# Attention scores as three one-pass products of split queries and keys, and fewer tiles for incoming weight words

## The chip, the cores and the metric

The kernel runs on one core of one Trainium2 chip. The metric is the device time of one execution in microseconds (us), median of three runs. A core has five engines that matter here: TensorE (PE) for matrix products, VectorE (DVE), ScalarE (ACT), GpSimd (POOL), and SyncE (SP), which starts the transfers (DMAs). Each works through its own instructions in the order in which they stand and waits for others by semaphores.

## The reference

Attention over 8 batches, 12 heads, 448 positions and head size 64, with the scores mixed across heads before the softmax and the weights mixed across heads after it; then a feed-forward block on all 3584 tokens.

```python
scores = scale * np.matmul(q, k.transpose(0, 1, 3, 2))
scores = np.einsum('bhij,hg->bgij', scores, w_pre)
scores = scores - np.max(scores, axis=-1, keepdims=True)
attn = np.exp(scores)
attn = attn / (np.sum(attn, axis=-1, keepdims=True) + 1e-09)
attn = np.einsum('bhij,hg->bgij', attn, w_post)
out = np.matmul(attn, v)
...
a = x @ w1
b = x @ w2
h = a * b @ w3
return (h @ w_out).astype(np.float32)
```

The weights of the feed-forward block arrive as 64-bit words and are turned into 32-bit floats on the chip.

## The kernel before, in words

The order of the work is written out by hand. `run` goes through 366 steps (`n`), two steps for each pair of tiles of ten query rows. In an even step the pair's row maxima (`largest`, L227, DVE) and exponentials (`exp`, L235, ACT) are issued; in an odd step PE gets the products with V (`av`, L301, when they are due), the head mixing after the softmax of the pair before (`post`, L260, tiles `pso`), the head mixing before the softmax of the next pair (`mix`, L220, tiles `psm`), and then the score units that a table `qks` puts into this step (`qk`, L174, tiles `psq`). The rest of the step's PE time goes to the feed-forward block (`eg`, `eo`, `e`, `e1o` to `e3o`; L522, L553, L702), so many matmuls in each step as a table `share` says. Those are 128x448 products of operands split into a rounded high part and a low rest (type fp32r): three one-pass products (`PAIRS`) instead of one full fp32 product. The program is thus one fixed order on each engine.

A **score unit** `(b, p, c)` computes, for batch `b` and the two heads of pair `p`, 128 rows of queries (`c` 0 to 2) against all 448 keys; `c` 3 takes the last 64 rows of two pairs at once. Head 0 has its 64 elements in rows 0 to 63 of the tile `kq`, head 1 in rows 64 to 127. Before, a unit is four fp32 matmuls with 64 rows and 64 columns of the array each: two heads times two halves of 64 queries. An fp32 matmul stands as two records in the trace, so a unit is eight records of `psq`. ACT copies its two banks out (`st`, L179 and L180), and SP stores them (`raw_d<-st`). SP loads `kq` (`load_kq`, L157) six steps ahead into four buffers.

The **weight words**: `ask_words` (L103) starts on SP the load of one piece of words (`cs<-w`) and appends it to a list; `converting` takes the oldest, lets ACT square the upper halves (`square`, L110, tile `cm`), DVE assemble the floats (L121 to L124), and, a step later, ACT and POOL split them (`two_parts`, L129 and L130), after which SP stores the parts (`w_d<-wu`, L425). The first 40 pieces (`5 * KF`) belong to the folded weights and are done by step 50; 32 pieces of `w1` and `w2` follow. The list is filled up to `DEEP` (5) pieces in five buffers of tag `s`. Later `sums` uses buffers of the same tag for combinations of weights: ACT casts (L483), POOL subtracts (L484), SP stores (`s_d<-s`, L486).

Of the kernel before, what the change touches and what calls it, by code (L numbers as in the profile page):

```python
# [15 lines left out]
B, H, S, D = 8, 12, 448, 64  # L16
DM, FF = 768, 1024
HP = H // 2
# [3 lines left out]
QT, NJ = 128, 4  # L22
GB = 15
NG = NB // GB
KF, K1 = FF // 128, DM // 128
IH = IB // 2
HK = H * IH
PP = 64
# [3 lines left out]
CW = 384  # L32
DH = DM // 2
LATE = 2 * NB + GB + 2
PAIRS = ((0, 0), (0, 1), (1, 0))
N_UP, NS = 20, 50
DEEP = 5
ONE = 2


# [10 lines left out]
class Kernel:  # L51
# [43 lines left out]

    def ask_words(self, depth):

        while len(self.asked) < depth and self.sources:
            src, n = self.sources.pop(0), self.n_words
            s = self.cs.tile([128, CW, 2], I32, tag="s", name=f"cs{n}", bufs=DEEP)  # L100
            a, k = src.shape[1], src.shape[2] // 2
            s = s[:, :a * k]
            self.nc.sync.dma_start(s.rearrange("p (a n) b -> p a (n b)", a=a), src)  # L103
            self.asked.append(s)
            self.n_words += 1
# [26 lines left out]
    def converting(self, jobs, late=False):  # L132
# [22 lines left out]
    def load_kq(self, b, p):  # L155
        t = self.kp.tile([128, 2 * S], F32, tag="kq", name=f"kq{b}_{p}", bufs=4)
        self.nc.sync.dma_start(t, self.kq[b, p].rearrange("p a j -> p (a j)"))  # L157
        self.kqs[b, p] = t

    def parts(self, b, p, c):  # L160
        pairs = ((p, 2 * c), (p, 2 * c + 1)) if c < 3 else ((p - 1, 6), (p, 6))
        if b == 0:
            return [(self.kqs[0, p], j * PP + S * (j > 1), QT) for p, j in pairs]
        return [(self.kqs[b, p], j * PP, S) for p, j in pairs]

    def qk(self, b, p, c, banks):


        nc = self.nc
        ps = [self.bank(i, f"psq{b}_{p}_{c}_{s}")[:, :S] for s, i in enumerate(banks)]  # L170
        for z, (t, q, k) in enumerate(self.parts(b, p, c)):
            for s in range(2):
                rows = slice(s * D, (s + 1) * D)
                nc.tensor.matmul(ps[s][z * PP:(z + 1) * PP], t[rows, q:q + PP], t[rows, k:k + S], start=True, stop=True)  # L174
        if b == c == 0:
            st = self.sz[:, 2 * p:2 * p + 2]
        else:
            st = (self.qp if b == 0 and p % 2 else self.kp).tile([128, 2, S], F32, tag="st", name=f"st{b}_{p}_{c}", bufs=2)
        nc.scalar.copy(st[:, 0], ps[0])  # L179
        (nc.vector.tensor_copy if b == c == 0 else nc.scalar.copy)(st[:, 1], ps[1])  # L180
        raw = self.raw_d[b]
        if c == 3:
            def store():
                for z in range(2):
                    nc.sync.dma_start(raw[3 * QT:, 2 * (p + z) - 2:2 * (p + z)], st[z * PP:(z + 1) * PP])
            return store
        n = QT if b or c else FIRST
        return lambda: nc.sync.dma_start(raw[c * QT:c * QT + n, 2 * p:2 * p + 2], st[:n])
# [280 lines left out]
    def sums(self, w, f, k):  # L469


        nc, n = self.nc, k * 128
        y = self.ys.pop((w, f))[:, :, :n]

        def sum(out, a, b, op):
            nc.vector.tensor_tensor(out, a, b, op=op)

        def split(m, i):
            s = self.cs.tile([128, CW, 2], I32, tag="s", name=f"s{w}_{f}_{m}", bufs=DEEP)
            s = s.rearrange("p n b -> p (n b)").bitcast(F32)  # L480
            dst, x = self.s_d[w][m][f].rearrange("p (t n) -> p t n", t=2), y[:, i]
            hi, lo = s[:, :n], s[:, n:2 * n] if w < 2 else x
            nc.scalar.copy(hi.bitcast(F32R), x)  # L483
            nc.gpsimd.tensor_tensor(lo.bitcast(F32R), x, hi, op=ALU.subtract)  # L484
            if w < 2:
                self.later.append(lambda: nc.sync.dma_start(self.s_d[w][m][f], s))  # L486
            else:
                self.later.append(lambda: nc.sync.dma_start(dst[:, 0], hi))
                self.later.append(lambda: nc.sync.dma_start(dst[:, 1], lo))

        def first():
            sum(y[:, 0:2], y[:, 0:2], y[:, 2:4], ALU.subtract)

        def second():
            sum(y[:, 1:3], y[:, 1:3], y[:, 0::3], ALU.add)

        def third():
            sum(y[:, 3], y[:, 3], y[:, 0], ALU.subtract)
# [242 lines left out]
    def run(self):  # L741
        nc, tc = self.nc, self.tc
# [33 lines left out]
        w = self.kp.tile([128, 2, S], F32, tag="st", name="wpre_s", bufs=2)[:, 0, :PP]  # L776
# [29 lines left out]

        loads, qks, avs = {}, {}, {}
        for n, u in enumerate([(0, p, c) for c in (1, 2) for p in range(HP)] + [(0, p, 3) for p in range(1, HP, 2)]):  # L810
            qks[n] = [u]
        for b in range(1, B):
            first, per = (11, 28 / 21) if b == 1 else ((b - 1) * NB - 6, NB / 21)
            units = [(b, p, c) for g in range(0, HP, 2) for p, c in [*itertools.product((g, g + 1), range(3)), (g + 1, 3)]]
            for i, (b, p, c) in enumerate(units):
                n = int(first + i * per) | (b > 1)
                qks.setdefault(n, []).append((b, p, c))
                if c == 0:
                    loads.setdefault(max(n - 6, 0), []).append((b, p))
        for b in range(B):  # L820
            for a in range(NG):
                for g in range(HP):
                    n = (b * NB + (a + 1) * GB + 3) | 1
# [65 lines left out]
        for n in range(N + 6):  # L889
# [4 lines left out]
            if n == SWITCH:  # L894
                assert done == total
                next(background, None)
                self.do_ends()
                self.do_soon()
                self.do_later()
                assert not fold_pieces  # L900
                self.close("fp")
                self.wp = self.pool("wp", 5, side="right")
                self.up = self.pool("up", 1, side="right")
                self.xp.append(self.pool("xp1", 1, side="right"))
                background, total, done = self.experts(phases), (E_1 + E_2) * ONE + P_1 * (B - ONE) // 2, 0
# [18 lines left out]
            m, odd = divmod(n, 2)  # L924
# [44 lines left out]
            self.do_ends()  # L969
            if not odd and m < SETS:  # L970
                self.exp(m)
            advance(now - now // 2)
            for x in avs.get(n, []):
                self.av(*x)
# [33 lines left out]
def words(w):  # L1008

    import numpy as np  # L1010
    return np.ascontiguousarray(w).view(np.int64)


def layouts(inputs):
    import numpy as np
    q, k, v = inputs["q"], inputs["k"], inputs["v"]
    qt = q.transpose(0, 1, 3, 2).reshape(B, HP, 2, D, S)
    kt = k.transpose(0, 1, 3, 2).reshape(B, HP, 2 * D, S)
    kq = np.ascontiguousarray(np.stack([qt.reshape(B, HP, 2 * D, S), kt], axis=3))
# [32 lines left out]
```

## Time and profile before

| what | value |
|---|---|
| median of 3 runs | 1441.87 us (1441.68 to 1443.87) |
| the profiled execution, its own time | 1437.83 us |
| its span, first to last instruction | 1436.1 us |
| mean granted TensorE clock | 0.986 |
| busy: PE, DVE, ACT, POOL | 1382.4, 741.1, 832.4, 620.3 us |
| from 220 to 376 us: 31 squares of weight words, DMA share | 17.64 us busy, 0.95 |

A row of the profile's groups gives line, engine, operation, output and inputs, the array's rows and columns for PE, and the count; then busy time and mean duration in ns. A row of the timeline gives start, duration, the same names and, in brackets, idle time ahead of it with what ended it. Matmuls are pipelined: what one costs is the distance between starts, not its duration.

### The profile page before, as it was taken

How to read it: one execution, taken by the hardware profiler on the slowest of the kernel's cores; microseconds unless marked ns; L12 is line 12 of the kernel's file. 1: busy time of each engine (PE TensorE's matmuls, PEld its weight loads, DVE VectorE, ACT ScalarE, POOL GpSimd, SP SyncE). 2: the span in 40 equal slices, each digit the busy share in tenths (PEclk: the TensorE clock that was granted, in tenths of full speed). 3: DMA queues.
4: the chain of work that ended last, by engine and by line, in shares of the span. 5: the costliest groups of instructions: out<-in, count | busy, mean ns of one | idle time of the engine just before them, and what ended most of it. 6: DMA issues, size and time to landing. Idle time of an engine off the chain costs nothing.

```text
span 1436.1 us, 45775 instructions
## 1 busy us (share of the span) xinstructions
PE 1382.4 (96%) x18684; PEld 1055.2 (73%) x18684; DVE 741.1 (52%) x1497; ACT 832.4 (58%) x1952; POOL 620.3 (43%) x754
## 2 busy tenths in 40 slices
PE   5889999999999999999999999999999999999998
PEld 2457786776677667776777777777777777899988
DVE  6867566767544544432444436334444446345563
ACT  4867666777766666665656556556555445422231
POOL 2433233434433544532345336334335446446693
PEclk7989999999999999999999999999999999999999
DMA  8998789999999999999989979799879757698775
GB/s 294 366 326 279 236 270 322 320 312 317 324 286 348 355 356 330 362 346 349 287 275 290 320 259 280 249 323 354 288 229 281 241 177 223 195 337 270 231 232 171
DMA packets 203761, 416.87 MB, mean 290 GB/s; under 512 B 20528, under 2 KB 120112, under 8 KB 203472
## 3 DMA queue, kind: packets, MB, share of 16 engines
q1 hardware_dynamic: 203552, 413.94, 87.6%
q8 instruction: 149, 2.44, 0.7%
q14 instruction: 60, 0.49, 0.1%
HBM read 279.77 MB, written 134.09 MB: 288 GB/s over the span
## 4 chain that ended last, share of the span: by engine, by line
PE 82%; DMA 8%; DVE 4%; ACT 2%; issue 1%; POOL 1%; SPq 0%; DVEq 0%; POOLq 0%; ACTq 0%
PE e L702 21%; PE psa L301 11%; PE pso L260 10%; PE psm L220 9%; PE psq L174 7%; PE eg L522 5%; PE psf L360 4%; PE eo L553 4%; PE e2o L702 4%; PE e1o L702 4%; PE e3o L702 4%; DMA wu<-w_d 3%; DMA r<-raw_d 2%; DMA raw_d<-st 2%; ACT e L235 1%
## 5 line engine op out<-in xcount | busy, mean ns | idle before, releaser
L247 POOL TENSOR_SCALAR w<-wpo,ri 128x60 f32<-128x60 f32 x360 | 180.7, 518 | 485.1 <-DVE ri L245 465.3
L227 DVE TENSOR_REDUCE mn<-psm 128x1 f32<-128x448 f32 x360 | 207.7, 618 | 321.6 <-PE psm L220 321.3
L274 ACT COPY mt<-pso 128x480 f32<-128x480 f32 x352 | 197.9, 621 | 185.8 <-PE pso L260 185.6
L702 PE MATMUL e<-eh,wu 128*128 128x448 f32 x1008 | 296.8, 371 | 6.4 <-DVE c L656 3.2
L235 ACT ACTIVATE e<-psm,mn 128x448 f32<-128x448 f32 x360 | 226.8, 643 | 7.9 <-DVE mn L227 7.9
L702 PEld LDWEIGHTS e<-eh,wu 128*128 128x128 f32 x1008 | 187.5, 188 | 52.2 <-issue 26.8
L260 PEld LDWEIGHTS pso<-w,e 60*64 60x64 f32 x10080 | 175.2, 135 | 51.0 <-issue 42.5
L220 PE MATMUL psm<-r,wsc 60*64 60x448 f32 (+1 forms) x1440 | 191.2, 550 | 19.1 <-DVE cx L124 8.3
L260 PE MATMUL pso<-w,e 60*64 60x60 f32 x10080 | 199.1, 224 | 0.4 <-ACT mt L274 0.3
L702 PE MATMUL e<-el,wu 128*128 128x448 f32 x504 | 186.9, 371 | 0.0
L301 PE MATMUL psa<-mt,v 128*64 128x150 f32 (+1 forms) x2304 | 156.9, 292 | 4.1 <-ACT st L179 4.1
L301 PEld LDWEIGHTS psa<-mt,v 128*64 128x64 f32 x2304 | 143.6, 137 | 20.1 <-ACT st L179 6.7
L174 PE MATMUL psq<-kq 64*64 64x448 f32 x1176 | 154.6, 542 | 2.4 <-ACT st L179 2.4
L656 DVE TENSOR_TENSOR c<-c,e 128x448 f32<-128x448 f32 x168 | 101.7, 618 | 87.7 <-PE e L702 82.9
L179 ACT COPY st<-psq 128x448 f32<-128x448 f32 x162 | 86.4, 533 | 73.7 <-ACT mt L274 34.1
L522 PE MATMUL eg<-xh,wu 128*128 128x448 f32 x384 | 119.2, 381 | 6.3 <-DMA wu<-w_d 6.3
L641 POOL TENSOR_TENSOR el<-x,eh 128x448 fp32r<-128x448 f32 x90 | 103.7, 1170 | 32.8 <-ACT eh L640 29.9
L702 PEld LDWEIGHTS e<-el,wu 128*128 128x128 f32 x504 | 94.6, 188 | 22.5 <-issue 14.1
L174 PEld LDWEIGHTS psq<-kq 64*64 64x64 f32 x1176 | 60.8, 135 | 56.4 <-issue 28.8
L522 PEld LDWEIGHTS eg<-xh,wu 128*128 128x128 f32 x384 | 71.9, 190 | 38.7 <-issue 24.0
L244 DVE TENSOR_SCALAR sa<-sm 128x2 f32<-128x2 f32 x180 | 34.9, 194 | 113.6 <-ACT e L235 113.1
L180 ACT COPY st<-psq 128x448 f32<-128x448 f32 x162 | 87.6, 541 | 0.0
(99 smaller groups left out, 2010.1 us busy)
## 6 DMA issues: line engine op xcount, KB each, us to landing
r<-raw_d SPq DMA_DIRECT2D x344, 210.0 KB, 5.1
raw_d<-st SPq DMA_DIRECT2D x138, 448.0 KB, 6.1
wu<-w_d SPq DMA_DIRECT2D x104, 384.0 KB, 6.7
wu<-s_d SPq DMA_DIRECT2D x96, 384.0 KB, 4.8
wu<-w_d SPq DMA_DIRECT2D x51, 512.0 KB, 5.5
kq<-kq SPq DMA_DIRECT2D x42, 448.0 KB, 7.0
wu<-s_d SPq DMA_DIRECT2D x36, 512.0 KB, 4.9
x<-x_d SPq DMA_DIRECT2D x72, 224.0 KB, 5.7
```

The lines of the kernel that those rows point to most:

```text
L174: nc.tensor.matmul(ps[s][z * PP:(z + 1) * PP], t[rows, q:q + PP], t[rows, k:k + S], start=True, stop=True)
L220: nc.tensor.matmul(ps[s][c * PP:(c + 1) * PP, :S], self.wsc[k], r[k, c], start=True, stop=True)
L227: self.nc.vector.tensor_reduce(mn[:, s:s + 1], self.psm[m][s][:, :S], axis=AX.X, op=ALU.min)
L235: nc.scalar.activation(e, p[:, :S], AF.Exp, bias=mn[:, s:s + 1], scale=-1.0, accum_out=sm[:, s:s + 1])
L247: nc.gpsimd.tensor_scalar_mul(w2[:, s], self.wpo, ri[:, s:s + 1])
L260: nc.tensor.matmul(self.pso[c][z * PP:(z + 1) * PP, at:at + HK], e[k, j * PP:(j + 1) * PP], w2s[k, s], start=True, stop=True)
L274: self.nc.scalar.copy(dst.rearrange("p j g (s i) -> p j s g i", s=2), src)
L301: nc.tensor.matmul(self.psa[rows, g % 3, :W], v[:, j, rows], mt[:, j, 2 * g + s, :W], start=(j == 0), stop=(j == NJ - 1))
L522: nc.tensor.matmul(p, u[:, k % (K1 // 2), x], xs[y][:, k], start=(k == 0 and t == 0), stop=(k == K1 - 1 and t == 2))
L641: nc.gpsimd.tensor_tensor(lo, x, hi.bitcast(F32), op=ALU.subtract)
L656: nc.vector.tensor_tensor(a[out], a[to[0]], p, op=ALU.add)
L702: nc.tensor.matmul(p, w[:, k, x], ops[m, k][y], start=(k == 0 and t == 0), stop=(k == nk - 1 and t == 2))
```

## The change: what it does

It has three parts.

1. From batch 2, pair 2 on (`PARTED`), units with `c` 0 to 2 are done as three products of split operands. A new step `split_kq`, three steps ahead of a pair's first such unit, lets ACT round 832 columns of `kq` (384 queries and 448 keys) to fp32r (`kh`) and POOL subtract the rounded values in two pieces of 416 columns (`kl`). A unit is then six matmuls: high with high, high with low, low with high, each for two heads, with 64 rows and 128 columns of the array each. The two heads lie in the two row halves. 102 units change, with 34 splits; 49 later units with `c` 3 and the earlier ones stay.
2. In these pairs the unit with `c` 3 comes first, and both loads of `kq` are started six steps ahead of it. The queries are stored by the host with the last 64 rows first.
3. The buffers of the words: three in `cs`, and two more in the pool `fp`, which is closed at step 50. Once 40 pieces have been asked for, the list is filled up to two pieces (`KEPT - 1`) instead of five. `sums` has three buffers instead of five.

```diff
+DEEP, KEPT = 5, 3
+PARTED = (2, 2)
...
-        while len(self.asked) < depth and self.sources:
+        while len(self.asked) < (depth if self.n_words < 5 * KF else KEPT - 1) and self.sources:
             src, n = self.sources.pop(0), self.n_words
-            s = self.cs.tile([128, CW, 2], I32, tag="s", name=f"cs{n}", bufs=DEEP)
+            kept = n % DEEP < KEPT or n >= 5 * KF
+            s = (self.cs if kept else self.fp).tile([128, CW, 2], I32, tag="s", name=f"cs{n}", bufs=KEPT if kept else DEEP - KEPT)
...
+    def split_kq(self, b, p):
+        x = self.kqs[b, p][:, PP:]
+        n = 2 * S - PP
+        hi = self.kh.tile([128, n], F32R, tag="kh", name=f"kh{b}_{p}")
+        lo = self.kp.tile([128, 2 * S], F32R, tag="kq", name=f"kl{b}_{p}", bufs=4)[:, :n]
+        self.nc.scalar.copy(hi, x)
+        for half in (slice(0, n // 2), slice(n // 2, n)):
+            self.nc.gpsimd.tensor_tensor(lo[:, half], x[:, half], hi[:, half].bitcast(F32), op=ALU.subtract)
+        self.kqs[b, p, "parts"] = hi, lo
...
+        if c < 3 and (b, p) >= PARTED:
+            t = self.kqs[b, p, "parts"]
+            for n, (x, y) in enumerate(PAIRS):
+                for s in range(2):
+                    rows = slice(s * D, (s + 1) * D)
+                    nc.tensor.matmul(ps[s], t[x][rows, c * QT:(c + 1) * QT], t[y][rows, 3 * QT:],
+                                     start=(n == 0), stop=(n == 2))
...
-            s = self.cs.tile([128, CW, 2], I32, tag="s", name=f"s{w}_{f}_{m}", bufs=DEEP)
+            s = self.cs.tile([128, CW, 2], I32, tag="s", name=f"s{w}_{f}_{m}", bufs=KEPT)
...
+                units += [(b, *x) for x in ([(g + 1, 3), *three] if (b, g) >= PARTED else [*three, (g + 1, 3)])]
...
+                elif c == 3:
+                    loads.setdefault(n - 6, []).extend([(b, p - 1), (b, p)])
+                elif c == 0:
+                    splits[n - 3] = b, p
...
+            if n in splits:
+                self.split_kq(*splits[n])
```

On PE, around one unit of batch 2, pair 3 (`psq2_3_1`), the order before is this; `psm` is the mixing that stands ahead of the unit and `eg` the feed-forward product behind it.

```order
L260 MATMUL pso1_142<-w230_3594,e30_1_3585 64x60
L220 MATMUL psm32_0_3765<-r32_3566,wsc_138 64x448
L220 MATMUL psm32_1_3766<-r32_3566,wsc_138 64x448
L220 MATMUL psm32_0_3765<-r32_3566,wsc_138 64x448
L220 MATMUL psm32_1_3766<-r32_3566,wsc_138 64x448
L174 MATMUL psq2_3_1_0_3774<-kq2_3_3321 64x448
L174 MATMUL psq2_3_1_1_3775<-kq2_3_3321 64x448
L174 MATMUL psq2_3_1_0_3774<-kq2_3_3321 64x448
L174 MATMUL psq2_3_1_1_3775<-kq2_3_3321 64x448
L522 MATMUL eg0_1_1_3691<-xl0_1261,wu6_3563 128x448
```

The same unit after the change, one pair of tiles later:

```order
L282 MATMUL pso1_142<-w231_3719,e31_1_3699 64x60
L242 MATMUL psm33_0_3898<-r33_3674,wsc_138 64x448
L242 MATMUL psm33_1_3899<-r33_3674,wsc_138 64x448
L242 MATMUL psm33_0_3898<-r33_3674,wsc_138 64x448
L242 MATMUL psm33_1_3899<-r33_3674,wsc_138 64x448
L189 MATMUL psq2_3_1_0_3907<-kh2_3_3594 128x448
L189 MATMUL psq2_3_1_1_3908<-kh2_3_3594 128x448
L189 MATMUL psq2_3_1_0_3907<-kl2_3_3595,kh2_3_3594 128x448
L189 MATMUL psq2_3_1_1_3908<-kl2_3_3595,kh2_3_3594 128x448
L189 MATMUL psq2_3_1_0_3907<-kh2_3_3594,kl2_3_3595 128x448
L189 MATMUL psq2_3_1_1_3908<-kh2_3_3594,kl2_3_3595 128x448
L544 MATMUL eg0_1_1_3705<-xh0_1260,wu7_3671 128x448
```

Four matmuls with 64 columns became six with 128. Each of the 102 changed units stands alone in this way, with `psm` ahead of it and a feed-forward matmul behind it.

On SP, in the stage of the 32 late words, the order before is this; `r` is the fetch for a pair of tiles, `raw2_d` the store of a score unit, `wu4` the unit made of word piece 44, `cs50` the load of piece 50.

```order
L188 DMA raw2_d_64<-st2_2_0_3382 128x896
L425 DMA w0_d_70<-wu4_3385 128x768
L103 DMA cs50_3421<-w2 128x3x256
L202 DMA r31_3478<-raw1_d_63 60x2x448 x2
L188 DMA raw2_d_64<-st2_2_1_3472 128x896
L425 DMA w0_d_70<-wu5_3475 128x768
L103 DMA cs51_3508<-w2 128x3x256
```

After the change:

```order
L447 DMA w0_d_70<-wu4_3387 128x768
L105 DMA cs47_3424<-w2 128x3x256
L224 DMA r31_3483<-raw1_d_63 60x2x448 x2
L210 DMA raw2_d_64<-st2_2_0_3477 128x896
L447 DMA w0_d_70<-wu5_3480 128x768
L105 DMA cs48_3513<-w2 128x3x256
```

Behind the store of unit 4 stood the load of piece 50, and now stands that of piece 47: the load of a piece moved three pieces later. ACT squares piece 46 at that place, and piece 47 next.

More of the change, by code (lines that the diff above doesn't have):

```diff
@@ L36 @@
 N_UP, NS = 20, 50
-DEEP = 5
+DEEP, KEPT = 5, 3
+PARTED = (2, 2)
 ONE = 2
@@ L163, in parts @@
             return [(self.kqs[0, p], j * PP + S * (j > 1), QT) for p, j in pairs]
-        return [(self.kqs[b, p], j * PP, S) for p, j in pairs]
+        return [(self.kqs[b, p], (j + 1) * PP % S, S) for p, j in pairs]
     def qk(self, b, p, c, banks):
@@ L170, in qk @@
         ps = [self.bank(i, f"psq{b}_{p}_{c}_{s}")[:, :S] for s, i in enumerate(banks)]
[L171 to L174, printed above, removed]
+        if c < 3 and (b, p) >= PARTED:
[5 more added lines that the diff above has]
+                                     start=(n == 0), stop=(n == 2))
+        else:
+            for z, (t, q, k) in enumerate(self.parts(b, p, c)):
+                for s in range(2):
+                    rows = slice(s * D, (s + 1) * D)
+                    nc.tensor.matmul(ps[s][z * PP:(z + 1) * PP], t[rows, q:q + PP], t[rows, k:k + S],
+                                     start=True, stop=True)
         if b == c == 0:
@@ L805, in run @@
         held = lambda: nc.sync.dma_start(self.raw_d[0][FIRST:QT], self.sz[FIRST:])
-        loads, qks, avs = {}, {}, {}
+        loads, qks, avs, splits = {}, {}, {}, {}
         for n, u in enumerate([(0, p, c) for c in (1, 2) for p in range(HP)] + [(0, p, 3) for p in range(1, HP, 2)]):
@@ L813, in run @@
             first, per = (11, 28 / 21) if b == 1 else ((b - 1) * NB - 6, NB / 21)
-            units = [(b, p, c) for g in range(0, HP, 2) for p, c in [*itertools.product((g, g + 1), range(3)), (g + 1, 3)]]
+            units = []
+            for g in range(0, HP, 2):
+                three = [*itertools.product((g, g + 1), range(3))]
+                units += [(b, *x) for x in ([(g + 1, 3), *three] if (b, g) >= PARTED else [*three, (g + 1, 3)])]
             for i, (b, p, c) in enumerate(units):
@@ L817, in run @@
                 qks.setdefault(n, []).append((b, p, c))
-                if c == 0:
-                    loads.setdefault(max(n - 6, 0), []).append((b, p))
+                if (b, p) < PARTED:
+                    if c == 0:
+                        loads.setdefault(max(n - 6, 0), []).append((b, p))
+                elif c == 3:
+                    loads.setdefault(n - 6, []).extend([(b, p - 1), (b, p)])
+                elif c == 0:
+                    splits[n - 3] = b, p
         for b in range(B):
@@ L901, in run @@
                 self.close("fp")
+                self.kh = self.pool("kh", 2, side="right")
                 self.wp = self.pool("wp", 5, side="right")
@@ L1018, in layouts @@
     kt = k.transpose(0, 1, 3, 2).reshape(B, HP, 2 * D, S)
-    kq = np.ascontiguousarray(np.stack([qt.reshape(B, HP, 2 * D, S), kt], axis=3))
+    qr = qt.reshape(B, HP, 2 * D, S)
+    kq = np.ascontiguousarray(np.stack([np.concatenate([qr[..., 3 * QT:], qr[..., :3 * QT]], axis=3), kt], axis=3))
     q0 = qt[0].reshape(HP, 2 * D, S)
```

## The prediction

> **What bounds the kernel now.** I read the page's head first, then busy time by stages, then the chain of waits at one place.
>
> ```profile
> span 1436.1 us, 45775 instructions
> PE 1382.4 (96%) x18684; PEld 1055.2 (73%) x18684; DVE 741.1 (52%) x1497; ACT 832.4 (58%) x1952; POOL 620.3 (43%) x754
> PE 82%; DMA 8%; DVE 4%; ACT 2%; issue 1%; POOL 1%; SPq 0%; DVEq 0%; POOLq 0%; ACTq 0%
> 200.00:300.00 100.00, 96.43 (x1529) 70.15 (x1527) 66.60 (x144) 71.24 (x173) 36.32 (x52) 1.00 0.94 312
> 500.00:600.00 100.00, 96.04 (x1464) 71.39 (x1465) 50.53 (x106) 65.90 (x157) 49.71 (x57) 0.98 1.01 349
> 800.00:900.00 100.00, 99.68 (x1474) 75.97 (x1473) 48.00 (x101) 59.98 (x140) 47.31 (x58) 1.00 0.88 283
> ```
>
> The stage rows give PE, weight load, DVE, ACT and POOL busy, then granted clock, DMA share and GB/s. PE is busy for 96 to nearly 100 of each 100 us, the chain that ended last is 82% PE, and the clock is full. So PE time added to a unit arrives at the end in full, and so does every wait that reaches PE. Between 200 and 300 us ACT is at 71% and the DMAs at 0.94: that is the tight stage.
>
> **The units.** The chain shows what a unit is worth, and the PE timeline around it what a change of the array's shape costs (start, duration).
>
> ```profile
> 606.05 0.76 PE psm L220 x8
> 606.81 0.75 PE psq L174 x8
> ```
>
> ```profile
> 606.59 0.98 PE L174 MATMUL psq<-kq 64*64 64x448 f32 x8
> 607.50 0.47 PE L522 MATMUL eg<-xl,wu 128*128 128x448 f32 x1
> 607.81 0.56 PE L522 MATMUL eg<-xh,wu 128*128 128x448 f32 x2
> 608.21 0.37 PE L522 MATMUL eg<-xl,wu 128*128 128x448 f32 x1
> ...
> 610.44 0.36 PE L553 MATMUL eo<-eh,wu 128*128 128x448 f32 x1
> 610.64 0.37 PE L553 MATMUL eo<-el,wu 128*128 128x448 f32 x1
> 610.94 0.28 PE L260 MATMUL pso<-w,e 60*64 60x60 f32 x4
> ```
>
> Within one shape a one-pass 128x448 matmul follows the last by 0.20 us ((608.21 - 607.81) / 2). From 128*128 to 64-row, 64-column tiles the distance is 0.30 (610.64 to 610.94): 0.10 lost. From `psq` to `eg` it is 607.50 - 606.59 = 0.91 where the unit is worth 0.75: 0.16 lost, and the first `eg` then holds the next up for 0.31 instead of 0.20, because its 128 weight columns could not be loaded ahead: 0.11 more. From `psm` to `psq`, the same shape, nothing is lost.
>
> After the change each of the 102 units is 64 rows by 128 columns, a third shape, between `psm` and a feed-forward product. Does a change of columns alone empty the array? The row that is nearest has 128 rows on both sides, and 128 columns, then 64:
>
> ```profile
> 601.27 0.56 PE L522 MATMUL eg<-xh,wu 128*128 128x448 f32 x2
> 601.76 3.28 PE L301 MATMUL psa<-mt,v 128*64 128x150 f32 x48
> ```
>
> The second `eg` starts at 601.27 + 0.20 = 601.47 and `psa` 0.29 later, not 0.20: it does. So I take the full loss on both sides. Counted from where `psq` would start: 0.16 until the first pair can start; 0.31 to the second pair; 0.20 to the third; 0.30 to `eg`; 0.31 to the second `eg`: 1.28 us. Before, the same stretch is 607.81 - 606.59 = 1.22. The unit gets 0.06 us dearer, although its arithmetic falls from 0.75 to about 3 x 0.20 = 0.60. 102 x 0.06 = **+6.1 us**.
>
> Two things here no row shows. That both row halves run side by side in one pass is taken from `psq`, where two heads share 0.75. If they ran one after the other, three more distances of 0.20 make it 102 x 0.60 = 61 us more. If on the other hand the array need not empty when the row halves stay, the first pair starts at once and the unit's end loses 0.10 and 0.11 as now: 0.60 + 0.10 + 0.11 = 0.81 against 0.75 + 0.16 + 0.11 = 1.02, a gain of 0.21, or 21 us. The term lies between -21 and +67, and I take +6.1, by the `eg` to `psa` row.
>
> The Trainium skill, "TensorEngine Tiling (Array Packing)", section Key Properties, says that changing the tiling mode, and not just the tile, drains TensorE. That rule speaks against this change; by it the term is +6.1 and the gain of 21 us cannot come. The same skill, "TensorE: Matmul & The Clock Gate", gives a warm distance of N / 2.4 + 2.5 ns, 189 ns for 448 columns, where the rows here have 0.20; by it, with 0.02 saved at the one plain distance and some 0.01 at two others, the term would be an estimated +2 us.
>
> **The words.** Before, the load of a piece stands four squares ahead of its use, after the change one. A load takes this long (count, KB, median us to landing; `wu<-s_d` has the same size):
>
> ```profile
> cs<-w SPq DMA_DIRECT2D x32, 384.0 KB, 7.0
> wu<-s_d SPq DMA_DIRECT2D x96, 384.0 KB, 4.8
> s_d<-s SPq DMA_DIRECT2D x32, 384.0 KB, 6.9
> ```
>
> The squares are this far apart (31 of them in 156 us, then two neighbours on ACT, with what stands between):
>
> ```profile
> 220.00:376.00 156.00, 17.64 (x31) 1.00 0.95 319
> ```
>
> ```profile
> 272.22 0.57 ACT L110 ACTIVATE cm<-cs 128x384 f32<-128x384 f32 x1
> ...
> 274.93 0.56 ACT L110 ACTIVATE cm<-cs 128x384 f32<-128x384 f32 x1
> 275.39 1.11 ACT L274 COPY mt<-pso 128x480 f32<-128x480 f32 x2
> ...
> 279.09 0.64 ACT L235 ACTIVATE e<-psm,mn 128x448 f32<-128x448 f32 x1 [1.34 <-DVE mn L227]
> ...
> 280.33 0.56 ACT L110 ACTIVATE cm<-cs 128x384 f32<-128x384 f32 x1
> ```
>
> SP starts a load close to the square that stands beside it:
>
> ```profile
> 272.80 0.40 SPq L103 DMA_DIRECT2D cs<-w  x1
> ...
> 275.95 0.39 SPq L103 DMA_DIRECT2D cs<-w  x1
> ```
>
> Today each of these loads is used four squares later. After the change the load at 272.80 is the one that the square at 274.93 needs, and with 7.0 us it lands at 279.8. ACT would stand there for 4.9 us with the copies `mt`, `st` and the exponentials (279.09) queued behind it, and PE's next mixing waits for those exponentials:
>
> ```profile
> 279.87 1.22 PE L220 MATMUL psm<-r,wsc 60*64 60x448 f32 x5 [0.28 <-ACT e L235]
> ```
>
> That mixing already waits for ACT, so little hides it: ACT's idle 1.34 us.
>
> Sum: 156 / 31 = 5.0 us between squares on average, so a load comes 7.0 - 5.0 = 2.0 us late. The wait helps the next piece, whose load SP has started already; with even distances only half of it is left: 30 x 2.0 / 2 = 30 us. Uneven distances as above make it more, ACT's idle time takes some back, and as the stage gets longer the DMAs get quicker, towards the 4.8 of the second row; at 4.8 only pieces close behind another wait, a quarter of the 30 perhaps, for 4.8 - 2.7 = 2.1 us each less half for the idle time, 8 us. Without the halving it is 60. I take **+22 us** (8 to 48), nearer to the even sum since the 7.0 is the transfer itself. All of it falls between 220 and about 400 us.
>
> **The splits.** Nearest rows for the ACT copy of 832 columns and the two POOL pieces of 416:
>
> ```profile
> L179 ACT COPY st<-psq 128x448 f32<-128x448 f32 x162 | 86.4, 533 | 73.7 <-ACT mt L274 34.1
> L641 POOL TENSOR_TENSOR el<-x,eh 128x448 fp32r<-128x448 f32 x90 | 103.7, 1170 | 32.8 <-ACT eh L640 29.9
> ```
>
> By columns ACT gets 533 x 832 / 448 = 990 ns at most, 34 times: 34 us; POOL 2 x 1170 x 416 / 448 = 2.17 us, 34 times: 74 us. POOL's 620 us leave room, and the first unit needs the result three steps later. On ACT seven of the 34 stand in the stage of the words, ahead of copies that PE needs; half of those seven reach PE, 3.5 us, while behind 60% busy I count the rest at nothing. **+3.5 us** (0 to 12, if a third of all do). The loads of `kq` keep their number; two now start together, beside a DMA share of 0.94, and I count that at nothing.
>
> **The sums.** `s` is written again after three casts instead of five.
>
> ```profile
> 570.36 0.54 ACT L483 CAST s<-y 128x384 fp32r<-128x384 f32 x1
> ...
> 579.20 0.53 ACT L483 CAST s<-y 128x384 fp32r<-128x384 f32 x1
> ```
>
> ```profile
> 574.90 0.34 SPq L486 DMA_DIRECT2D s_d<-s  x1
> ```
>
> The cast at 579.20 is the third behind that at 570.36, whose store is started at 574.90 and lands 6.9 later, at 581.8: a wait of 2.6 us on ACT. If a third of the 44 casts wait 2 us, ACT loses 29 us at 66% busy, and I let a sixth reach PE: **+5 us** (0 to 12).
>
> **The sum.** 6.1 + 22 + 3.5 + 5 = 36.6 us. The profiled execution took 1437.83 us, with 1.7 around its span; the median of the runs stands 4.04 above it, at 1441.87. So 1474.4 beside the profiled one, and **1478.5** for the median. A measurement here tells about 0.2% (2.9 us) from no change.
>
> **The rivals.**
>
> *No emptying between 64-row shapes.* For it: no row shows these two shapes side by side. Against it: `eg` to `psa`. The price is -21 us. It decides, and the kernel gets faster, where the other three terms stay under 18; with these at their low ends, 8 + 0 + 0, the time is 1441.9 - 21 + 8 = 1429. With the words at 22 it ends at 1441.9 - 21 + 30.5 = 1451.
>
> *ACT's gaps take the words' waits.* For it: ACT is busy only 71% of that stage, and the words are needed only some units later. Against it: `psm` waits for the exponentials in the row at 279.87. Then the units and a little of the rest are left: 6 + 4, 1452.
>
> *The row halves run one after the other*, or not in one pass. For it: no one-pass matmul with 64 rows is in the trace. Against it: `psq` shares them in fp32, and `eg` is of the same type in one pass. 1478.5 + 61 = 1540.
>
> **How the numbers follow.** My forecast has 0.62, words hidden 0.13, no emptying 0.15 (half of it below 1439, half near 1451), row halves in turn 0.06, and 0.04 for what I have not thought of, most of it faster. Faster by over 0.2% comes to 0.07 and some of the words' case where ACT's copies cost less than the rows say, with the unknown: 0.13; within 0.2%: 0.07 from the same two cases; slower: 0.80. The range leaves out the faster cases and the row halves in turn: low 1442 from the words' case at its best; high 1478.5 + 26 (words at 48) = 1504.
>
> **What would show it.** Each step has its place in the profile after: the chain's `psq` piece, and the distance from `psm` to the first changed `psq` (0.16 longer than now if the array empties); ACT's waits at L112 for `cs<-w` between 220 and 420 us, with PE's `psm` waiting for ACT behind them, and the last square later than 376 us by about 22; ACT's waits at L505 for `s_d`. I am wrong if L112 shows no wait, if a changed unit and the `eg` behind it take under 1.2 us, or if the two heads' matmuls do not start together.

## The result, and the profile after

The changed kernel took 1480.83 us (median of 4 runs, 1477.68 to 1484.87), the kernel before, on the same chip, 1442.53 (1441.68 to 1443.87). The ratio is 1.0269, interval 1.0244 to 1.0294: slower by 38.8 us, 35 to 42. The profiled execution took 1477.68 us.

From the page of the changed kernel, its span, the engines' busy time and the chain by engine:

```profile
span 1475.9 us, 45488 instructions
PE 1405.2 (95%) x18480; PEld 1072.6 (73%) x18480; DVE 760.4 (52%) x1497; ACT 859.9 (58%) x1986; POOL 694.1 (47%) x822
PE 75%; DMA 12%; ACT 4%; DVE 3%; POOL 3%; issue 3%; SPq 1%; POOLq 0%; ACTq 0%; DVEq 0%
```

The span is 39.8 us longer. PE's share of the chain that ended last fell from 82% to 75%, and DMA's rose from 8% to 12%. PE has 204 fewer matmul records than before and is yet busy for 23 us more. Fewer instructions that take longer: that is the first sign of a lower clock.

To see where the time went, I compare the start of the same step's row maxima (L249, before L227) in the two traces. At step 52 the changed kernel is 0.63 us behind, at step 100 it is 35.25, and at the end 39.8. So 34.6 us are lost in the 48 steps in which the late words are turned into floats. The last operation of the assembly of a piece, one row from the kernel before and one from the changed one (durations min/median/max in ns, then first and last start), gives the end of that stage:

```profile
L124 DVE SCALAR_TENSOR_TENSOR cx<-cm,cx x72: 425/559/1331, 12.3 to 376.6; 128x384 f32<-128x384 f32 x64, 128x256 f32<-128x256 f32 x8
```

```profile
L126 DVE SCALAR_TENSOR_TENSOR cx<-cm,cx x72: 425/559/1374, 13.4 to 411.9; 128x384 f32<-128x384 f32 x64, 128x256 f32<-128x256 f32 x8
```

The last piece comes 35.3 us later. Busy time by window, over this stage, of the kernel before and then of the changed one (length, PE, weight load, DVE, ACT and POOL busy with counts, granted clock, DMA share, GB/s):

```profile
228.00:377.00 149.00, 143.84 (x2263) 101.53 (x2259) 106.95 (x228) 112.45 (x269) 61.96 (x83) 1.00 0.96 322
```

```profile
228.00:412.00 184.00, 161.02 (x2230) 111.57 (x2223) 110.56 (x228) 119.53 (x279) 75.48 (x98) 0.92 0.84 268
```

Two things changed. PE stands idle for 184.00 - 161.02 = 23.0 us, where it was 5.2: 17.8 more. And PE is busy for 17.2 us more with a like number of matmuls, at a clock of 0.92 where it was 1.00. The clock is 0.50 for 30.7 us of these 184, and PE is busy for 28.8 of them, so some 14 of the 17.2 us are the clock's. The DMAs are less busy (0.84), and a load of a piece lands in 5.2 us in the median where it took 7.0: the transfers are not short of bandwidth, they are started too late.

The waits by engine over the whole run of the changed kernel (total us, times, longest), and PE's row of the kernel before:

```profile
ACT cm L112 <- DMA cs<-w: 34.0, 19, 4.7
ACT s L505 <- DMA s_d<-s: 7.0, 5, 3.3
```

```profile
PE psm L242 <- ACT e L257: 19.9, 12, 3.4
```

```profile
PE psm L220 <- ACT e L235: 7.2, 9, 2.0
```

ACT now waits 19 times for the words of `w1` and `w2`, which it did not do before, and PE's mixing `psm` waits nearly three times as long for ACT's exponentials. One stretch of the changed kernel's timeline shows both ways in which such a wait arises, by SP, ACT, POOL, DVE and PE:

```profile
345.62 0.39 SPq L105 DMA_DIRECT2D cs<-w  x1
```

```profile
350.63 0.55 ACT L112 ACTIVATE cm<-cs 128x384 f32<-128x384 f32 x1 [1.99 <-DMA cs<-w]
351.09 0.62 ACT L257 ACTIVATE e<-psm,mn 128x448 f32<-128x448 f32 x1
...
353.09 0.52 ACT L131 CAST wu<-cx 128x384 fp32r<-128x384 f32 x1
...
359.99 0.64 ACT L257 ACTIVATE e<-psm,mn 128x448 f32<-128x448 f32 x1 [3.33 <-DVE mn L249]
```

```profile
353.27 2.13 POOL L170 TENSOR_TENSOR kl<-kq,kh 128x416 fp32r<-128x416 f32 x2 [3.55 <-ACT kh L168]
355.34 1.03 POOL L132 TENSOR_TENSOR wu<-cx,wu 128x384 fp32r<-128x384 f32 x1
```

```profile
356.40 0.47 DVE L123 TENSOR_SCALAR cx<-cs 128x384 int32<-128x384 int32 x1 [3.27 <-POOL wu L132]
...
359.33 1.15 DVE L249 TENSOR_REDUCE mn<-psm 128x1 f32<-128x448 f32 x2
```

```profile
351.85 1.22 PE L242 MATMUL psm<-r,wsc 60*64 60x448 f32 x5 [2.47 <-ACT e L257]
...
360.76 2.38 PE L242 MATMUL psm<-r,wsc 60*64 60x448 f32 x8 [2.66 <-ACT e L257]
```

First, the load started at 345.62 is the one that ACT needs at 348.64; ACT waits 1.99 us, the exponentials behind it start at 351.09, and PE has stood for 2.47 us at 351.85. Second, the two `kl` pieces of a split go first on POOL. The words' subtraction `wu` could start when ACT's cast ended at 353.61 and starts at 355.34. DVE needs it to free a buffer of `cx`, so it begins the next piece at 356.40, the row maxima queued behind it come at 359.33, the exponentials at 359.99, and PE has stood for 2.66 us at 360.76. Nothing on DVE, ACT or POOL is the bound. They are a ring, and PE hangs on it.

### The profile page after: what moved, and what is told of

It reads as the page before. It is cut to its first block, busy times and chain, and to the rows that moved or that the text cites. A ratio compares the mean times of both kernels' runs of the same rounds, so it can differ in the third digit from the quotient of the medians.

```text
span 1475.9 us, 45488 instructions
## 1 busy us (share of the span) xinstructions
PE 1405.2 (95%) x18480; PEld 1072.6 (73%) x18480; DVE 760.4 (52%) x1497; ACT 859.9 (58%) x1986; POOL 694.1 (47%) x822
## 4 chain that ended last, share of the span: by engine, by line
PE 75%; DMA 12%; ACT 4%; DVE 3%; POOL 3%; issue 3%; SPq 1%; POOLq 0%; ACTq 0%; DVEq 0%
PE e L724 19%; PE psa L323 10%; PE pso L282 9%; PE psm L242 8%; PE psq L189 4%; PE eg L544 4%; PE psf L382 4%; PE e1o L724 4%; PE e2o L724 4%; PE e3o L724 4%; DMA cs<-w 3%; PE eo L575 3%; PE psq L195 2%; DMA wu<-w_d 2%; ACT e L257 2%
## 5 line engine op out<-in xcount | busy, mean ns | idle before, releaser
L249 DVE TENSOR_REDUCE mn<-psm 128x1 f32<-128x448 f32 x360 | 207.7, 619 | 305.4 <-PE psm L242 305.2
L269 POOL TENSOR_SCALAR w<-wpo,ri 128x60 f32<-128x60 f32 x360 | 175.3, 505 | 370.5 <-DVE ri L267 357.1
L257 ACT ACTIVATE e<-psm,mn 128x448 f32<-128x448 f32 x360 | 227.0, 643 | 15.5 <-DVE mn L249 15.5
L242 PE MATMUL psm<-r,wsc 60*64 60x448 f32 (+1 forms) x1440 | 198.9, 559 | 30.5 <-ACT e L257 19.9
L544 PE MATMUL eg<-xh,wu 128*128 128x448 f32 x384 | 123.5, 394 | 4.8 <-DMA wu<-w_d 4.8
L170 POOL TENSOR_TENSOR kl<-kq,kh 128x416 fp32r<-128x416 f32 x68 | 78.3, 1172 | 80.9 <-ACT kh L168 79.3
L266 DVE TENSOR_SCALAR sa<-sm 128x2 f32<-128x2 f32 x180 | 45.1, 251 | 116.8 <-ACT e L257 115.9
L544 PEld LDWEIGHTS eg<-xh,wu 128*128 128x128 f32 x384 | 75.5, 199 | 27.6 <-issue 14.8
L330 ACT COPY xd<-psa 128x450 f32<-128x450 f32 (+1 forms) x36 | 19.2, 534 | 117.5 <-PE psa L323 114.1
```

The source lines that it names most:

```text
L242: nc.tensor.matmul(ps[s][c * PP:(c + 1) * PP, :S], self.wsc[k], r[k, c], start=True, stop=True)
L249: self.nc.vector.tensor_reduce(mn[:, s:s + 1], self.psm[m][s][:, :S], axis=AX.X, op=ALU.min)
L257: nc.scalar.activation(e, p[:, :S], AF.Exp, bias=mn[:, s:s + 1], scale=-1.0, accum_out=sm[:, s:s + 1])
L269: nc.gpsimd.tensor_scalar_mul(w2[:, s], self.wpo, ri[:, s:s + 1])
L544: nc.tensor.matmul(p, u[:, k % (K1 // 2), x], xs[y][:, k], start=(k == 0 and t == 0), stop=(k == K1 - 1 and t == 2))
```

## The experiments

Eleven more kernels were run. Each ratio is against the kernel before, run beside it on the same chip; us are the ratio's excess times 1442.

| run | what differs | ratio (interval) | us |
|---|---|---|---|
| the change | all | 1.0269 (1.0244 to 1.0294) | +38.8 |
| e1_words | the change without its units and splits | 1.0212 (1.0199 to 1.0225) | +30.6 |
| e11_lead_one | before, word list of two | 1.0198 (1.0179 to 1.0217) | +28.6 |
| e12_lead_two | before, word list of three | 1.0058 (1.0041 to 1.0074) | +8.4 |
| e9_words_three | e1 with a list of three | 1.0061 (1.0038 to 1.0084) | +8.8 |
| e2_three | the change with a list of three | 1.0194 (1.0171 to 1.0217) | +28.0 |
| e4_onesplit | e2 with one split | 1.0085 (1.0068 to 1.0101) | +12.3 |
| e6_no_subtract | e2, POOL's pieces gone | 1.0046 (1.0029 to 1.0062) | +6.6 |
| e10_pieces_later | e2, POOL's pieces moved back | 1.0143 (1.0114 to 1.0171) | +20.6 |
| e13_late_units | e2, units and splits only behind the words | 1.0076 (1.0054 to 1.0097) | +11.0 |
| e7_fp32wide | e2, units in fp32, no splits | 1.0123 (1.0106 to 1.0141) | +17.7 |
| e8_stalls | before, with ACT held up eight times | 1.0343 (1.0319 to 1.0367) | +49.5 |

The kernel before stays the fastest of all; none of these beats it.

### The words: list of two, and of three

The first run drops units and splits from the change and keeps words, buffers and sums.

```diff
-PARTED = (2, 2)
+PARTED = (9, 9)
```

> The change to the word and sum buffers alone; the units stay four fp32 matmuls and there are no splits. Theory (the words' waits on ACT make most of the loss): 1442.5 + 30 = about 1472 us, ACT waits for cs<-w at L112 of about 34 us in all, the loss made between steps 52 and 100 as in the changed kernel. Rival (the units and splits make it, and the words' waits fall into time that ACT and PE had to spare): under 1447 us.

It keeps +30.6 of the +38.8 us and took 1473.11 us, as the theory had it. ACT waited 44.5 us for words at L112, more than expected, and 29.4 of the 32.4 us that its profiled execution is longer are lost between steps 52 and 100. Two runs then put the list alone into the kernel before, with its five buffers and its sums untouched:

```diff
-        while len(self.asked) < depth and self.sources:
+        while len(self.asked) < (depth if self.n_words < 5 * KF else 2) and self.sources:
```

> The kernel before the change with its five buffers, but the list of the 32 late words filled to two pieces: the lead of one square by itself. Theory (the lead makes nearly all of the loss that the buffers' change makes alone, 31 us): 1468 to 1473 us, waits at L110 for cs<-w of 35 us or more. Rival (the three buffers and the sums make a good part): 1460 us or less.

The same line with 3 for 2:

> The kernel before the change with its five buffers, and the list filled to three pieces: a lead of two squares without fewer buffers. Theory (the 9 us that three buffers with a lead of two cost are partly waits of unlucky words and partly the sums): 1445 to 1449 us. Rival (they are the lead alone): 1451 us or more. Other rival (they are the buffers alone): 1443 us or less.

And the three buffers with a list of three (e1 with `KEPT` for `KEPT - 1`):

> The word and sum buffers alone again, units and splits as before the change, with the list filled to three pieces. Theory (the words' lateness is cured by a lead of two squares; what stays are the sums): 1443 to 1447 us, no waits at L112 for late words to speak of. Rival (three buffers are too few whatever the lead): 1455 us or more.

ACT's wait for the words, in e11 and then in e12:

```profile
ACT cm L110 <- DMA cs<-w: 44.5, 17, 6.6
```

```profile
ACT cm L110 <- DMA cs<-w: 8.6, 2, 5.4
```

One list entry decides. e11 took 1471.30 us, inside its theory's range; e12 took 1451.38, which is its first rival's. With a load one square ahead 17 pieces are late, with two squares ahead two are, and the loss falls from 28.6 to 8.4 us. The number of buffers and the sums make little of it: e9 with three buffers costs what e12 costs with five, and e1 is 2.0 us above e11, within their intervals. e9 missed: it took 1454.73 us where 1443 to 1447 were expected, and ACT still waited three times for words, 11.1 us in all. What the theories gave to the sums, or to the buffers, does not show; the rival, the lead alone, stands.

### The splits: ACT's copy or POOL's pieces

With the words taken out of the way by a list of three, what do splits and units cost?

```diff
-        while len(self.asked) < (depth if self.n_words < 5 * KF else KEPT - 1) and self.sources:
+        while len(self.asked) < (depth if self.n_words < 5 * KF else KEPT) and self.sources:
```

> The changed kernel with the list of words filled up to three pieces instead of two, in the same three buffers, so that a load stands two squares ahead of its use. Theory: with two mean distances of 5.0 us ahead the 7 us load is there in time, and what is left is the units (102 x 0.05 = 5) and 3 for splits and sums: about 1450 us, waits at L112 under 5 us. Rival: no change that matters, 1478 us or more.

The theory of e2 missed: it expected 1450 us and 1468.72 came. Its waits for words are down (9.3 us, 2 times), so another cost had come up. Four kernels look for it. The first makes only the first split and lets all changed units use it, so the scores of the other pairs are left out. (Its `kl` also gets a tile of its own, where the others take one of the four `kq` buffers.)

```diff
...
-            t = self.kqs[b, p, "parts"]
+            t = self.kqs[2, 2, "parts"]
...
-            if n in splits:
+            if splits.get(n) == PARTED:
```

> As the kernel with three pieces, but one split instead of 34: all changed units use the operands of batch 2, pair 2, so the scores of the others are left out, while PE has the same 102 six-matmul units. Theory (a split costs 3.5 us over all, PE pays 0.05 a unit): 3 us less than with 34 splits, about 1447 us. Rival (the splits on ACT and POOL are what is left, the units cost nothing): about 1443 us.

The second keeps ACT's copies and drops POOL's subtraction; the rounded values stand in for the rests, so the low products are left out:

```diff
-        lo = self.kp.tile([128, 2 * S], F32R, tag="kq", name=f"kl{b}_{p}", bufs=4)[:, :n]
...
-        for half in (slice(0, n // 2), slice(n // 2, n)):
-            self.nc.gpsimd.tensor_tensor(lo[:, half], x[:, half], hi[:, half].bitcast(F32), op=ALU.subtract)
-        self.kqs[b, p, "parts"] = hi, lo
+        self.kqs[b, p, "parts"] = hi, hi
```

> Three pieces, 34 splits, but the POOL subtraction of the splits is left out: the rounded operands are used for the low parts too, so the scores lack their low products; ACT's rounding and PE's six matmuls stay. Theory (a split costs by POOL: its pieces stand ahead of the words' subtraction, for whose buffers DVE waits, and behind DVE the maxima and the exponentials): 1457 us or less, DVE's waits for POOL at L123 back to about 6 us. Rival (a split costs by the 0.9 us on ACT): 1466 us or more.

The third issues POOL's pieces at the end of the step, behind the words' subtraction where there is one in that step:

```diff
...
-            if n in splits:
-                self.split_kq(*splits[n])
+            low = self.split_kq(*splits[n]) if n in splits else []
...
+            for f in low:
+                f()
```

> Three pieces, and the POOL pieces of a split are issued at the end of the step, behind the words' subtraction of the same step, which four of the seven splits of the word stage stood ahead of. Theory (POOL ahead of the words): 4 to 8 us less than with three pieces alone, about 1463 us. Rival (ACT): no change, 1469 us.

The fourth starts units and splits at batch 3, pair 4 (`PARTED = (3, 4)`): 78 units and 26 splits, none beside the words.

> The changed kernel with three pieces, and the split units only from batch 3, pair 4 on, so that no split stands in the stage of the words: 78 changed units, 26 splits. Theory (a split costs much only where DVE and ACT wait for words and POOL works on them): the 9 us of three buffers, 78 x 0.05 = 4, and 2: about 1457 us. Rival (each of the 34 splits costs its 0.6 us wherever it stands): 26 x 0.6 more, 1471 us.

e4 missed its theory and its rival alike: it took 1455.37 us. Splits cost nearly 16 us in e2 (28.0 against 12.3 in e4). Without POOL's pieces (e6) the loss falls by 21.4 us though ACT's 34 copies stay, so the copies cost next to nothing. Moving the pieces of four of the seven early splits behind the words' subtraction (e10) gives 7.4 back, give or take 5. And the 26 later splits cost nothing that shows: e13's 11.0 us are e9's 8.8 and 78 units at 0.06, 13.5, within the intervals. The starts of the row maxima show the same: between steps 52 and 100 the profiled execution of e2 loses 21.4 us, that of e10 18.3, of e4 9.4, of e6 8.6 and of e13 6.0. (Those of e2 and e10 are the longest of their kernels' runs, 1476.47 and 1472.42 us; behind step 100 e2's loses 17.3 us more, e13's 10.8 and that of e9, which has no splits, 10.9.) The waits of e2 and then of e6 between 225 and 425 us show one way that the cost takes:

```profile
DVE cx L123 <- POOL wu L132: 16.7, 10, 3.2
```

```profile
ACT e L257 <- DVE mn L249: 13.7, 7, 3.7
```

```profile
PE psm L242 <- ACT e L257: 16.7, 9, 3.9
```

```profile
DVE cx L123 <- POOL wu L132: 10.6, 9, 1.6
```

```profile
ACT e L254 <- DVE mn L246: 4.1, 5, 1.4
```

```profile
PE psm L239 <- ACT e L254: 9.6, 7, 3.5
```

It is the ring of the stretch at 353 us above. Six microseconds less at POOL become ten less at ACT and seven less at PE, though DVE's waits at L123 stay at 10.6 us, above the 6 expected.

There is a second way, which e6 closes too and e10 does not: beside the `kl` pieces DVE's operations take longer. With the same 1497 instructions DVE is busy for 760.2 us in e2 and 739.9 in e6, and between steps 52 and 100 for 113.3 and 105.6. How the cost divides between POOL's queue and the slower DVE was not taken apart. A third possible way is not one: e4 and e6 also free the places that `kl` takes among the `kq` buffers, but in e2 SP stands ahead of a load of `kq` only once between 225 and 425 us, for 0.7 us.

The parts don't add up to the last microsecond: e6 is 5.7 us below e4, although it does more, and 8 below e9 and 102 units (8.8 + 6.1). I take it that a late piece makes the next one late, so that each part's price depends on the others; no run shows that by itself.

### The units: shape or type

The 102 units as plain fp32 with 64 rows and 128 columns, without splits:

```diff
+            t = self.kqs[b, p]
+            for s in range(2):
+                rows = slice(s * D, (s + 1) * D)
+                nc.tensor.matmul(ps[s], t[rows, PP + c * QT:PP + (c + 1) * QT], t[rows, S:], start=True, stop=True)
```

> Three pieces, no splits, and the 102 units as two full fp32 matmuls with 64 rows and 128 columns, one for each head: same type as the mixing ahead of them, other shape. Theory (a change of shape empties the array): first changed psq 0.47 us behind the last psm, not 0.31, a unit 0.21 us dearer than before (1.43 against 1.22), 102 x 0.21 = 21, and 2 for the sums: about 1465 us. Rival (it is the step from fp32 to one-pass fp32r that empties it): distance 0.31, about 1444 us.

On PE's timeline, the mixing ahead of the unit in the kernel before, then a changed unit of the kernel after, then one of e7:

```profile
605.83 0.54 PE L220 MATMUL psm<-r,wsc 60*64 60x448 f32 x1
```

```profile
642.86 0.97 PE L242 MATMUL psm<-r,wsc 60*64 60x448 f32 x7
643.77 0.47 PE L189 MATMUL psq<-kh 64*128 64x448 f32 x2
644.08 0.36 PE L189 MATMUL psq<-kl,kh 64*128 64x448 f32 x2
644.28 0.37 PE L189 MATMUL psq<-kh,kl 64*128 64x448 f32 x2
644.57 0.47 PE L544 MATMUL eg<-xl,wu 128*128 128x448 f32 x1
644.88 0.36 PE L544 MATMUL eg<-xh,wu 128*128 128x448 f32 x1
```

```profile
641.49 0.55 PE L240 MATMUL psm<-r,wsc 60*64 60x448 f32 x2
...
642.40 1.02 PE L188 MATMUL psq<-kq 64*128 64x448 f32 x4
643.36 0.47 PE L573 MATMUL eo<-el,wu 128*128 128x448 f32 x1
643.66 0.56 PE L573 MATMUL eo<-eh,wu 128*128 128x448 f32 x2
```

Before, `psq` starts 606.59 - 605.83 = 0.76 us behind `psm`. Both kernels here have 0.91, with the split type and with fp32 alike. So the 0.15 goes with the change of shape, as forecast, and not of type. The Trainium skill, "TensorEngine Tiling (Array Packing)", section Key Properties, says that a change of the tiling mode drains TensorE; the trace agrees, with that 0.15. From `psm` to the second feed-forward matmul it is 2.02 us after, 2.17 in e7 and 1.98 before. For e7 that is 0.19 x 102 = 19 us, and 17.7 came, its list of three included; the 8 us of e12 are not found again beside these units. Between steps 52 and 100 e7 loses 5.4 us, its longer units included, where e12 loses 8.6; why is open.

### What a wait costs: the clock

If PE loses more in a wait than the wait, then waits made on purpose, far from the words, should show it. The kernel before gets dummy copies on ACT ahead of the exponentials in eight steps, 16 to 44 of them:

```diff
+STALL = {n: 16 + 4 * ((n - 222) // 10) for n in range(222, 302, 10)}
...
+            for _ in range(STALL.get(n, 0)):
+                nc.scalar.copy(sc, self.wsc)
```

> The kernel before the change, with copies of 64 columns put on ACT ahead of the exponentials at eight places in steps 222 to 292, 16 at the first and 4 more at each further one (about 0.2 us each, so 3 to 9 us), far from words, splits and changed units. Theory (a wait of PE of 1.5 us or more also halves the granted clock for a stretch of 3.4 us or a multiple, which costs half of that again): the longer ones leave PE waiting for 1 to 5 us and are each followed by such a stretch; with 12 us of waits about 10 us come on top, 1464 us, mean clock under 1.00 in that stage. Rival (a wait costs its own length): clock 1.00 there, 1454 us.

The size was missed, since the waits came out longer than meant (up to 8.9 us between the starts of two matmuls). The mechanism holds. Steps 220 to 300, in the kernel before and then in e8:

```profile
768.00:1046.00 278.00, 277.44 (x4020) 211.95 (x4014) 119.17 (x261) 170.69 (x403) 123.98 (x160) 1.00 0.91 298
```

```profile
771.00:1101.00 330.00, 293.66 (x4023) 218.07 (x4018) 117.85 (x261) 228.21 (x644) 124.23 (x160) 0.93 0.78 251
```

These are the same matmuls on PE. The stage takes 52 us longer: PE is idle for 36.3 us instead of 0.6, and its work takes 16.2 us more, at a clock of 0.93. In the stretches at 0.50 PE is busy for 24.4 us, so some 12 of the 16.2 are the clock's. One of the eight waits, cut at the places where the clock changes:

```profile
893.88:897.30 3.42, 3.42 (x21) 2.90 (x23) 3.23 (x5) 3.13 (x12) 3.42 (x3) 1.00 1.01 313
897.30:900.71 3.41, 1.01 (x56) 0.88 (x56) 0.00 (x0) 3.00 (x14) 1.39 (x2) 1.00 0.91 317
900.71:907.54 6.83, 4.56 (x18) 2.00 (x19) 2.02 (x5) 4.33 (x14) 1.93 (x3) 0.50 0.15 45
907.54:910.95 3.41, 3.41 (x17) 2.90 (x16) 1.96 (x5) 2.92 (x8) 1.24 (x3) 1.00 0.81 240
```

PE is idle for 2.4 us of one stretch of 3.41 us, and is then granted half the clock for the next two. Two waits of the changed kernel, the first of them shown above, differ in just this:

```profile
350.26:353.67 3.41, 1.82 (x16) 0.81 (x16) 2.28 (x6) 2.97 (x7) 0.40 (x1) 1.00 0.72 234
353.67:357.09 3.42, 3.06 (x21) 2.06 (x18) 0.65 (x2) 2.84 (x6) 3.42 (x5) 1.00 0.00 0
```

```profile
316.13:319.54 3.41, 0.29 (x20) 0.16 (x10) 3.30 (x4) 0.50 (x1) 1.93 (x2) 1.00 0.99 264
319.54:326.37 6.83, 6.55 (x22) 3.93 (x23) 3.50 (x9) 5.48 (x15) 1.84 (x3) 0.50 0.95 295
```

The wait of 2.47 us that ended at 351.85 lies across a border of stretches, 1.59 us of it in the second, and the clock stays at 1.00. A wait of 3.40 us that ended at 319.82 fills the stretch before 319.54, and the clock is 0.50 for the next 6.83. The other wait shown above, up to 360.76, lies with 2.40 us in the stretch from 357.09 to 360.50, and it too is followed by 6.83 us at 0.50.

## Why the prediction came out as it did

The forecast was +36.6 us; +38.8 came. The two larger terms name the right waits, but that the total came within 2.2 us is luck: the words were put 6.6 us too low, and the splits and the sums together some 4.5 too high.

**The units: right.** 1.28 us was forecast from the place where `psq` would start to the second feed-forward matmul, against 1.22 before. Measured: 644.88 - (642.86 + 0.76) = 1.26. The steps are 0.15, 0.31, 0.20, 0.29 and 0.31, where 0.16, 0.31, 0.20, 0.30 and 0.31 stood. The two heads start 3 ns apart. Over the units with the same neighbours the median of the stretch from `psm` to the second feed-forward matmul is 2.02 us after and 1.97 before. And from step 100 to the end, behind the words, the lag grows by 4.6 us with 84 changed units. Both come to 0.05 each, or 5 to 6 us for the 102: the term stands. (Of the 66 other units 49 stand ahead of batch 2, pair 2, and 17, with `c` 3, behind it.) The rival without emptying and the one with row halves in turn are both refuted by these rows.

**The words: right in place and cause, 22 forecast, 28.6 measured** by the list alone (e11), inside 8 to 48. The chain is the one described: L112 waits, the exponentials stand behind it, `psm` waits. The step that failed is the pricing. The forecast counted each wait once, as idle time. In e11, between steps 52 and 100, PE idles for 15.5 us more than before, less than the 22, and its own work takes 13.4 us more, some 10 of them because it is busy for 20.3 us at half clock. In the changed kernel it is 17.8 and 17.2 us, as shown above. What e8 shows is that such waits lower the clock by themselves, with no words near. The lateness was sized wrongly too: in e11 the loads got quicker, as the forecast thought they might, to 5.2 us in the median, near the 4.8 at which it saw a loss of 8 us. Still 17 pieces kept ACT waiting, for 2.6 us on average. In the changed kernel the last assembly moved by 35 us instead of 22, with the splits and units of that stage in it.

**ACT's gaps take the words' waits: wrong here, but nearly right one square further.** PE's waits for the exponentials and its idle time above show that the gaps did not take them. With the load two squares ahead only two pieces wait on ACT, and 8.4 us are left (e12).

**The splits: +3.5 forecast, about +2 in the changed kernel** (38.8 less e1's 30.6 less 6.1, give or take 4), but by a step that was wrong. "POOL's 620 us leave room" is an average over the run. Where a `kl` pair of 2.1 us stands ahead of a word's subtraction, POOL is on the ring that PE waits for, and DVE, of which the term had nothing, is slowed beside it. ACT's copies, on which the term was built, take these rows' time and show no cost:

```profile
L168 ACT CAST kh<-kq 128x832 fp32r<-128x832 f32 x34 | 30.4, 893 | 0.0
L170 POOL TENSOR_TENSOR kl<-kq,kh 128x416 fp32r<-128x416 f32 x68 | 78.3, 1172 | 80.9 <-ACT kh L168 79.3 <-DVE cx L125 1.6
```

Their durations were forecast well (990 at most and 1086 ns each). With the list of three the same splits cost nearly 16 us. That in the changed kernel the words' waits cover the pieces, because whichever is later holds PE, is my reading of these totals; no run shows it by itself. Units, words and splits, as measured apart, come to 6 + 29 + 16 = 51 us, more than the 38.8 that the change costs.

**The sums: +5 forecast, 2 measured,** give or take 3 (e1 against e11, the three buffers included). ACT waits 5 times for `s_d`, 7.0 us in all, at 66% busy and far from PE.

Why a list of three still costs 8 us, with only two waits for words on ACT, is settled in part only. Between 227 and 385 us PE idles in e12 for 10.9 us, about 6 more than before in this stage, and the clock is 0.94; which of the early pieces sets that off was not taken apart. Nor is all of it lost there: the profiled execution of e12 loses 8.6 us between steps 52 and 100 and 3.0 behind, that of e9 8.3 and 10.9.

## What to carry to other kernels

Where waits leave PE idle for some 2 us at a time, as here, price a wait twice: as idle time, and as what the clock takes behind it. Read an engine's room in the stage, by the queue it stands in and by who waits for what is queued behind, not by its busy share over the run. And when a change has two costs that end at the same wait, take one away and measure again before you believe either to be small.

## What was new about the hardware

**The clock goes in stretches of 3.41 us.** In all 13 profiles the granted clock is 1.00 or 0.50 and changes only on a fixed grid of 3.413 us. I counted PE's idle time between matmuls in each stretch at full clock from 110 us on. After under 1.3 us idle the next stretch was never at half clock (4,907 stretches); after 1.3 to 2.0 us it was in 29 of 73; after over 2.0 us always (38 of 38). From half clock, 66 of 68 stretches with under 0.3 us idle were followed by full clock, and of 33 with more only one. What decides between 1.3 and 2.0 us is open. So a long wait costs itself and about 1.7 us more for each stretch at half clock in which PE works on; split by a border the same wait may cost nothing more, as at 350.26, where 1.59 us fell into the stretch. The Trainium skill, "TensorE: Matmul & The Clock Gate", section What's actually happening, speaks of a free-running window of about 3.4 us and of an idle window ahead of the lower clock. The grid agrees. That a whole window must be idle does not: anything over 2.0 of 3.41 us sufficed each time.

**DVE beside POOL.** The last operation of the assembly of a piece takes 0.56 us in the median and up to 1.37 (the two rows of L124 and L126 above; in the stretch at 357.51 the operation L125 took 1.24 beside POOL's subtractions). From 220 us on every one of them over 1.1 us overlapped work of POOL, though at 411.86 one took 0.56 beside it. The Trainium skill, "GPSIMD Engine Reference", section Specifications, says that it shares its SBUF interfaces with VectorE, with contention for VectorE's instructions that have two inputs there, among others; these operations have two, and the rows agree. Single operations were as slow before the change (1331 ns at most), but the `kl` pieces add to it: DVE is busy for 760.4 us after the change and was for 741.1, with as many instructions, and in the kernels without the pieces (e1, e6) it is 738.4 and 739.9.
